# Backward attention on one core: six transposes of E a step, X copied by VectorE, row factors by Pool, G in half tiles, and Z's sum behind the products

## The chip, the cores and the metric

The kernel runs on one core of one Trainium2 chip. TensorE (PE) multiplies matrices, VectorE (DVE) and ScalarE (ACT) work elementwise and can read PSUM, where PE writes, GpSimd (POOL) works on SBUF, and SyncE (SP) issues most of the DMAs. The metric is the device time in microseconds of one execution; a comparison takes the median of several. Lines (L629) are those of the kernel before.

## The reference, cut to what matters

The function is a transformer block with a gate, and the reference returns its output and seven gradients. With S = 2048 rows, D = 512, H = 32 heads of 16, F = 1792:

```python
xn = _layernorm(x)
s  = attention(xn, wqkv) @ wo          # softmax over 2048 keys for each head
g  = _silu(mlp(_layernorm(xn)))
out = x + s * g
out, vjp = jax.vjp(f, x, wqkv, wo, w1, b1, w2, b2);  grads = vjp(grad_out)
```

For each head the attention stage needs E = exp(q k^T - bound), its row sums L, O = E v / L, and for the gradients G = E * (dO v^T) elementwise, from which dq, dk and dv come. E and G are 2048 x 2048 for each of 32 heads; nothing of them is stored in HBM.

## The kernel before

Three stages follow one another. `phase_pre` makes the normalized inputs, the projections, the MLP and the packed operands of the attention; `attention_core` (L543) makes O, dq and the key and value gradients; `phase3` makes the outputs and weight gradients. Outside the attention a scheduler orders the instructions; inside it (`manual_schedule`, L913) each engine runs them in the order in which the code emits them. The change touches the attention, and two lines of `phase_pre` that set a sign.

**Work and order.** A pair is two heads; there are 16. A block is a pair and a quarter (512) of the queries: 64 blocks. A step `g` is a block and 128 keys (`kb`, 0 to 15), so a block has 16 steps, and there are 1024. A block starts with the step in which `g % 16` is 0. The loop at L839 emits, for each step, pieces of several steps at once, so that the stages overlap:

- `emit_s` (L629, L635): two products `s` (one for each head) of step g+1, into PSUM tiles of `ps_st`, and ACT's exp of them into `et`, which holds four steps of E in bf16.
- `emit_d` (L647): two products `d` of step g into `ps_d`. Together, the four products of 32 rows each use all of PE's rows.
- `emit_mult` (L660): DVE multiplies `d` and `et` into `gts`, which holds two steps of G.
- `emit_T` (L694): PE transposes of E into a tile `tT` of the same pool `ps_st` (three tiles for s, s and tT). Of each group of four steps, three of four query blocks `qb` are transposed on PE, eight transposes in one step, in three of four steps. `emit_cT` (L704): ACT copies tT to an `ek` tile.
- `emit_dmat` (L674, L678): SP issues a DMA transpose of G for each two steps (`gk`), and one of the fourth query block of E for each four steps.
- `emit_x` (L719, L722, L725): six products of step g-1 that sum X over the 16 steps in one PSUM tile: the row sums (part "l"), E with keys and values ("e"), and G with keys ("g"). Each writes 32 (or 17) partitions: "l" and "e" fill the four column groups of PE, "g" uses two.
- `emit_xs` (L734): at the block's end, ACT copies X to SBUF. `emit_XT` (L744) transposes the copy on PE in float32, in step 2 of the next block (`FIN_AT`), and `emit_fin` (L756 to L782) works out the row factors: DVE copies XT (`xt`), takes the reciprocal of L (`rL`), and makes `dl` and `ndr`; POOL makes the weights `W1` and `W2`, O and dq.
- `emit_z` (L804): the sum Z of the key and value gradients, of a block that ended some steps earlier: step g works on what `g + ZOFF` names (ZOFF = -21). Half of its steps (part 0) multiply W2 with transposed G, half (part 1) W1 with transposed E: four products of 32 x 512 each step, one for each column group. `emit_acc` (L819) adds Z to `acc` on DVE, twice a block, in the steps where eight Z steps are complete; Z has one PSUM tile.

The order within a step is written out by hand:

```python
        emit_z(g + ZOFF)
        emit_acc(g + ZOFF)
        emit_s(g + 1, 0)
        emit_XT(g)
        emit_d(g, 0)
        emit_d(g, 1)
        emit_s(g + 1, 1)
        emit_mult(g)
        emit_fin(g)
        emit_T(g)
        ...
        emit_xs(g - 1)
        emit_cT(g)
        emit_dmat(g)
```

`load_ops` (L577) loads a pair's operands with three DMAs and two DMA transposes (`KVT`, `QDT`) on SP, spread over 16 steps of the pair before.

Of the kernel before, what the change touches and what calls it, by code (L numbers as in the profile page):

```python
# [58 lines left out]
def phase_pre(ctx, tc, k, A_x, A_wqkv, A_wo, B_w1, B_b1, B_w2, B_b2, grad_out, dbg):  # L59
# [3 lines left out]
    with ExitStack() as c1:  # L63
# [52 lines left out]
        with ExitStack() as c0:  # L116
# [5 lines left out]
            for i in range(2):  # L122
                nc.gpsimd.memset(NS[i][:, :, :, :, 0:1], 1.0)
# [28 lines left out]
            for t in range(NT):  # L152
                pq = psA.tile([128, 512], f32, name="pq", tag="mm")
                for ic in range(IC):
                    nc.tensor.matmul(pq[:], lhsT=xnT[:, ic, t * 128:(t + 1) * 128], rhs=wqkv_sb[:, ic, 0:D],
                                     start=(ic == 0), stop=(ic == IC - 1))
                nq = NQ[(t // 4) % 2]
                qpv = nq[:, :, t % 4, :, :]
                nc.scalar.copy(out=qpv[:, :, :, 1:17], in_=pq[:].rearrange("p (a j c) -> p a j c", a=NPAIR, j=2))
                qq = qpv[:, :, :, 1:17]  # L160
                sq = wk.tile([128, H, DH], f32, name="sqq")
                nc.gpsimd.tensor_tensor(out=sq[:].rearrange("p (a j) c -> p a j c", j=2), in0=qq, in1=qq, op=ALU.mult)
                qn2 = wk.tile([128, H], f32, name="qn2")
# [379 lines left out]
def attention_core(ctx, tc, NAT_s, NATQ_s, Oall, dQall, dKVT_out, ident_f32, ident_bf, npairs=16, nqc=4):  # L543
# [9 lines left out]
    gbp = sb("gbp", 7)  # L553
    ekp = sb("ekp", 19)
    xsp = sb("xsp", 1)
    finp = sb("finp", 1)
    wp = sb("wp", 2)
# [17 lines left out]
    acc = opnd.tile([128, 2, 512], f32, name="acc")  # L575

# [87 lines left out]
    def emit_dmat(g):  # L664
        a = a_unit(g)
        if a is None:
            return
        j, kb = a
        kc = kb // 4
        if kb % 2 == 1:  # L670
            h = (kb // 2) % 2
            if h == 0:
                blk[j]["Gk"][kc] = gbp.tile([128, 2, 16, 128], bf16, name="gk")
            nc.sync.dma_start_transpose(out=blk[j]["Gk"][kc][:, h], in_=st_gt[g][:].rearrange("k a h q -> k (a h q)"))  # L674
        if kb % 4 == 3:
            ek = ekp.tile([128, 8, 128], bf16, name="ek")
            blk[j]["Ek"][(kc, 3)] = ek
            nc.sync.dma_start_transpose(out=ek[:], in_=st_et[g][:, 3].rearrange("k a h q -> k (a h q)"))  # L678

    def t_unit(g):  # L680
        a = a_unit(g - 4)
        if a is None or a[1] % 4 == 3:
            return None
        return a[0], a[1] // 4, a[1] % 4

    def emit_T(g):
        u = t_unit(g)
        if u is None:
            return
        j, kc, qb = u  # L690
        et = st_et[j * 16 + kc * 4 + 3]
        t = ps_st.tile([128, 8, 128], bf16, name="tT", tag="st")
        for b in range(8):
            nc.tensor.transpose(t[:, b, :], et[:, qb, b // 2, b % 2, :], ident_bf[:])  # L694
        st_T[g] = t

    def emit_cT(g):
        u = t_unit(g)
        if u is None:
            return  # L700
        j, kc, qb = u
        ek = ekp.tile([128, 8, 128], bf16, name="ek")
        blk[j]["Ek"][(kc, qb)] = ek
        nc.scalar.copy(out=ek[:].rearrange("q a k -> q (a k)").bitcast(f32),  # L704
                       in_=st_T.pop(g)[:].rearrange("q a k -> q (a k)").bitcast(f32))
# [22 lines left out]
    def emit_xs(g):  # L728
# [4 lines left out]
        xs = xsp.tile([128, 512], f32, name="xs")  # L733
        nc.scalar.copy(out=xs[:], in_=blk[j].pop("X")[:])  # L734
# [12 lines left out]
    def emit_fin(g):  # L747
# [7 lines left out]
        xt = finp.tile([128, 4, 128], f32, name="xt")  # L755
        nc.vector.tensor_copy(out=xt[:], in_=XT[:])  # L756
        XTv = xt[:].rearrange("q b (r c) -> q b r c", r=4)
        W1 = wp.tile([128, 4, 2, 32], bf16, name="W1")
        W2 = wp.tile([128, 4, 2, 32], bf16, name="W2")
        nc.gpsimd.memset(W2[:, :, :, 0:16], 0.0)  # L760
# [16 lines left out]
        nc.gpsimd.tensor_tensor(out=t1[:], in0=XTv[:, :, 0:2, 0:16], in1=bc(dl[:]), op=ALU.mult)  # L777
        nc.gpsimd.tensor_tensor(out=t1[:], in0=XTv[:, :, 2:4, 1:17], in1=t1[:], op=ALU.subtract)
# [4 lines left out]
        blk[j]["W1"] = W1  # L783
        blk[j]["W2"] = W2

    def emit_z(g):
# [7 lines left out]
        for par in range(2):  # L794
            kc = 2 * kp + par
            if part == 0:
                W = blk[j]["W2"]
                mv = blk[j]["Gk"][kc][:].rearrange("q a (r h b) k -> q h b a r k", r=2, h=2)[:, :, qb]
            else:
                W = blk[j]["W1"]  # L800
                mv = blk[j]["Ek"].pop((kc, qb))[:].rearrange("q (a h) k -> q h a k", h=2)
            for hj in range(2):
                r = 64 * par + 32 * hj
                nc.tensor.matmul(Z[r:r + 32, :], lhsT=W[:, qb, hj, :], rhs=mv[:, hj],  # L804
                                 start=(part == 0 and qb == 0), stop=(part == 1 and qb == 3), skip_group_check=True,
                                 tile_position=(0, r))

    def emit_acc(g):
# [11 lines left out]
        if qc == nqc - 1:  # L820
            if kp == 0:
                cur["ob"] = outp.tile([128, 2, 512], bf16, name="ob")
            ob = cur["ob"]
            nc.gpsimd.tensor_copy(out=ob[:, kp, :], in_=av)
            if kp == 1:
                def store():
                    dv = dKVT_out[p * 64:(p + 1) * 64, :].rearrange("r (a b s) -> r a b s", a=2, b=2)
                    for b in range(2):
                        nc.sync.dma_start(out=dv[:, :, b, :], in_=ob[b * 64:(b + 1) * 64])
                late.append((cur["g"] + 2, store))  # L830

    FIN_AT = 2
    ZOFF = -21
# [5 lines left out]
    for g in range(NSTEP + 16 + 8):  # L839
# [11 lines left out]
        emit_z(g + ZOFF)  # L851
        emit_acc(g + ZOFF)
        emit_s(g + 1, 0)
        emit_XT(g)
# [118 lines left out]
```

## Time and profile before

| what | us |
|---|---|
| median of 3 runs | 2687.34 (2686.54 to 2688.6) |
| the profiled execution, its own time | 2689.98 |
| span of its instructions | 2688.2 |
| attention stage, from the first s to the last Z | 283 to 2085 |
| in that stage: PE busy | 1703.65 of 1802 |
| in that stage: ACT busy | 1530.79 |
| in that stage: DVE busy | 1434.70 |
| in that stage: POOL busy | 249.69 |

The stage is two thirds of the time, and TensorE's clock is granted in full in it (1.00). A line of a group of instructions reads: line, engine, operation, output <- inputs, shapes, count | busy us in total, mean ns of one | idle time of the engine just before them, and what ended most of it. A line of the timeline reads: start in us, duration in us, engine, line, operation, count, and in brackets the idle time before and what released it. Matmuls overlap in the records, so the start of one to the start of the next says more than a duration.

### The profile page before, as it was taken

How to read it: one execution, taken by the hardware profiler on the slowest of the kernel's cores; microseconds unless marked ns; L12 is line 12 of the kernel's file. 1: busy time of each engine (PE TensorE's matmuls, PEld its weight loads, DVE VectorE, ACT ScalarE, POOL GpSimd, SP SyncE). 2: the span in 40 equal slices, each digit the busy share in tenths (PEclk: the TensorE clock that was granted, in tenths of full speed). 3: DMA queues.
4: the chain of work that ended last, by engine and by line, in shares of the span. 5: the costliest groups of instructions: out<-in, count | busy, mean ns of one | idle time of the engine just before them, and what ended most of it. 6: DMA issues, size and time to landing. Idle time of an engine off the chain costs nothing. (4 is left out here: it accounts for less than half of the span.)

```text
span 2688.2 us, 61100 instructions
## 1 busy us (share of the span) xinstructions
PE 2294.1 (85%) x24005; PEld 1054.0 (39%) x24064; DVE 1898.4 (71%) x3190; ACT 1795.7 (67%) x3317; POOL 600.7 (22%) x990
## 2 busy tenths in 40 slices
PE   3788799999999999999999999999999656656967
PEld 2333244444444444444444444444444333322433
DVE  5766687878788778787787877778787368860144
ACT  3344688888888888888888888888887254430110
POOL 0434111011110111101111011110111258850034
PEclk8899899999999999999999999999999878878989
DMA  5343999999999999999999999999999633327331
GB/s 188 94 128 126 186 199 212 195 211 204 204 216 193 211 204 204 215 196 215 201 202 215 191 214 202 205 209 198 210 198 182 229 109 103 103 72 185 116 111 43
DMA packets 1564740, 477.08 MB, mean 177 GB/s; under 512 B 1484706, under 2 KB 1549603, under 8 KB 1564451
## 3 DMA queue, kind: packets, MB, share of 16 engines
q1 hardware_dynamic: 1491058, 419.56, 78.5%
q10 hardware_dynamic: 73392, 53.62, 6.5%
q8 instruction: 188, 3.08, 0.5%
q14 instruction: 102, 0.83, 0.1%
HBM read 65.41 MB, written 55.32 MB: 45 GB/s over the span
## 5 line engine op out<-in xcount | busy, mean ns | idle before, releaser
L660 DVE TENSOR_TENSOR gts<-d,et 128x512 bf16<-128x512 f32 x2048 | 1292.3, 683 | 364.1 <-PE s L629 200.1
L635 ACT ACTIVATE et<-s 128x512 bf16<-128x512 f32 x2048 | 1127.3, 596 | 247.9 <-PE s L629 136.7
L629 PE MATMUL s<-QDT,KVT 32*128 32x512 bf16 x2048 | 528.0, 386 | 17.7 <-DMA QDT<-Pad 16.1
L647 PE MATMUL d<-QDT,KVT 32*128 32x512 bf16 x2048 | 489.9, 383 | 54.0 <-DVE gts L660 53.7
L694 PE MATMUL tT<-ident_bf,et 128*128 128x128 bf16 x6144 | 475.2, 220 | 40.1 <-ACT ek L704 39.4
L704 ACT COPY ek<-tT 128x512 f32<-128x512 f32 x768 | 455.2, 593 | 0.5 <-PE tT L694 0.5
L694 PEld LDWEIGHTS <-et 128*128 128x128 bf16 x6144 | 354.2, 98 | 213.1 <-issue 199.2
L722 PE MATMUL X<-et,NAT 128*32 128x512 bf16 x2048 | 404.0, 392 | 0.0
L719 PE MATMUL X<-et,Lc 128*32 128x512 bf16 x2048 | 403.4, 391 | 0.0
L725 PE MATMUL X<-gts,NAT 128*17 128x512 bf16 x2048 | 393.4, 380 | 0.0
L629 PEld LDWEIGHTS <-KVT 32*128 32x128 bf16 x2048 | 145.3, 91 | 555.1 <-issue 523.8
L804 PE MATMUL Z<-ek,W 128*32 128x512 bf16 x2048 | 300.8, 380 | 0.0
L804 PE MATMUL Z<-gk,W 128*32 128x512 bf16 x2048 | 289.6, 380 | 1.3 <-DVE acc L819 1.3
L771 POOL TENSOR_TENSOR W<-NATQq,rL 128x128 bf16<-128x128 bf16 x64 | 25.7, 401 | 1178.3 <-DVE rL L766 1178.3
L804 PEld LDWEIGHTS <-W 128*32 128x32 bf16 x4096 | 199.7, 96 | 125.9 <-issue 31.2
L719 PEld LDWEIGHTS <-Lc 128*32 128x32 bf16 x2048 | 98.2, 93 | 139.0 <-issue 59.6
L647 PEld LDWEIGHTS <-KVT 32*128 32x128 bf16 x2048 | 96.0, 91 | 11.4 <-issue 11.4
L722 PEld LDWEIGHTS <-NAT 128*32 128x32 bf16 x2048 | 98.6, 93 | 0.0
L421 PE MATMUL dh_tp<-ident_bf,dh 128*128 128x128 bf16 x224 | 31.0, 278 | 77.9 <-DVE dh L418 75.5
L725 PEld LDWEIGHTS <-NAT 128*17 128x17 bf16 x2048 | 95.3, 90 | 0.0
L448 PE MATMUL ps_dw<-dm_all,hgc 128*128 128x512 bf16 x220 | 54.0, 402 | 29.6 <-DMA hgc<-HG_s 29.4
L427 PE MATMUL ps_dy<-w1T,dh1T 128*128 128x512 bf16 x208 | 67.8, 471 | 3.7 <-ACT dh1T L422 3.4
(197 smaller groups left out, 2442.2 us busy)
## 6 DMA issues: line engine op xcount, KB each, us to landing
gk<-gts SPq DMA_TRANSPOSE x512, 4.2
HG_s<-hg SPq DMA_DIRECT2D x16, 448.0 KB, 2.9
DH_s<-dh ACTq DMA_DIRECT2D x16, 448.0 KB, 2.5
NAT<-NAT_s SPq DMA_DIRECT2D x16, 264.0 KB, 3.3
GB_s<-gB ACTq DMA_DIRECT2D x16, 256.0 KB, 2.0
ek<-et SPq DMA_TRANSPOSE x256, 3.1
dKVT_s<-ob SPq DMA_DIRECT2D x32, 128.0 KB, 2.5
dhc<-DH_s ACTq DMA_DIRECT2D x2, 2048.0 KB, 13.7
```

The lines of the kernel that those rows point to most:

```text
L427: nc.tensor.matmul(ps[:], lhsT=dh1T[:, fc, :], rhs=w1T[:, fc, :], start=(fc == 0), stop=(fc == FC - 1))
L448: nc.tensor.matmul(ps[:], lhsT=hgc[:, t, :], rhs=dm_all[:, t, :], start=(t == 0), stop=(t == NT - 1))
L629: nc.tensor.matmul(s[:], lhsT=op["KVT"][r:r + 32, kb * 128:(kb + 1) * 128], rhs=op["QDT"][r:r + 32, qc * 512:(qc + 1) * 512], start=True, ...
L635: nc.scalar.activation(out=et[:, :, kb % 4, hj, :], in_=s[:].rearrange("k (b q) -> k b q", b=4), func=ACT.Exp)
L647: nc.tensor.matmul(d[:], lhsT=op["KVT"][r:r + 32, kb * 128:(kb + 1) * 128], rhs=op["QDT"][r:r + 32, qc * 512:(qc + 1) * 512], start=True, ...
L660: nc.vector.tensor_tensor(out=gts[:, kb % 2, hj, :].rearrange("k (b q) -> k b q", b=4), in0=st_d.pop((g, hj))[:].rearrange("k (b q) -> k b ...
L694: nc.tensor.transpose(t[:, b, :], et[:, qb, b // 2, b % 2, :], ident_bf[:])
L704: nc.scalar.copy(out=ek[:].rearrange("q a k -> q (a k)").bitcast(f32), in_=st_T.pop(g)[:].rearrange("q a k -> q (a k)").bitcast(f32))
L719: nc.tensor.matmul(X[64 + 32 * hj:96 + 32 * hj, :], lhsT=Lc[:], rhs=et[:, :, kb % 4, hj, :], start=(kb == 0), stop=False, skip_group_check ...
L722: nc.tensor.matmul(X[32 * hj:32 * hj + 32, :], lhsT=NATt[:, kb, hj, 1:33], rhs=et[:, :, kb % 4, hj, :], start=(kb == 0), stop=(kb == 15), ...
L725: nc.tensor.matmul(X[64 + 32 * hj:64 + 32 * hj + 17, :], lhsT=NATt[:, kb, hj, 0:17], rhs=st_gt[g][:, kb % 2, hj, :], start=False, stop=(kb ...
L804: nc.tensor.matmul(Z[r:r + 32, :], lhsT=W[:, qb, hj, :], rhs=mv[:, hj], start=(part == 0 and qb == 0), stop=(part == 1 and qb == 3), skip_ ...
```

## The change

Eight things change in `attention_core`:

- **Transposes.** Every step transposes three query blocks of its own 128 keys for two heads (six transposes), one step later than its exp, in place of eight on three steps of four. ACT copies 128 x 384 (float32 words) each step into a part of a larger `ek` tile (pool `ekc`, six tiles); the DMA transposes of the fourth query block have a pool of their own (`ekd`, six tiles).
- **Order of a step.** The transposes come first behind s and d, then XT, then Z, then the X products; before, Z came first in the step and XT between s and d. `emit_mult` and `emit_fin` come behind them, and `emit_acc` behind `emit_xs`.
- **X.** DVE copies it to SBUF, behind the products of its step; before, ACT did.
- **Row factors.** POOL makes `ndl` and `ndr`; the sign that `ndr` carried is put into the operands (the first column of NAT is -1, and u of the queries is positive).
- **W1 and W2** have two fixed tiles each, and the zeros of W2 are written once.
- **G** has a tile for each two steps (half of before's tile), 13 of them for 7; Z's part 0 uses eight products of 32 x 256 for four of 32 x 512.
- **Z** begins a step earlier in the block's count (ZOFF = -20).
- **The results** of each half of `acc` are stored by themselves: four DMAs of 64 KB a pair in place of two of 128 KB.

```diff
-                nc.gpsimd.memset(NS[i][:, :, :, :, 0:1], 1.0)
+                nc.gpsimd.memset(NS[i][:, :, :, :, 0:1], -1.0)
...
-                nc.vector.tensor_scalar(out=qpv[:, :, :, 0], in0=u[:].rearrange("p (a j) -> p a j", j=2), scalar1=-1.0, scalar2=None,
-                                        op0=ALU.mult)
+                nc.vector.tensor_copy(out=qpv[:, :, :, 0], in_=u[:].rearrange("p (a j) -> p a j", j=2))
...
-    gbp = sb("gbp", 7)
-    ekp = sb("ekp", 19)
+    gbp = sb("gbp", 13)
+    ekd = sb("ekd", 6)
+    ekc = sb("ekc", 6)
...
-            h = (kb // 2) % 2
-            if h == 0:
-                blk[j]["Gk"][kc] = gbp.tile([128, 2, 16, 128], bf16, name="gk")
-            nc.sync.dma_start_transpose(out=blk[j]["Gk"][kc][:, h], in_=st_gt[g][:].rearrange("k a h q -> k (a h q)"))
+            gk = gbp.tile([128, 2, 2, 4, 128], bf16, name="gk")
+            blk[j]["Gk"][kb // 2] = gk
+            nc.sync.dma_start_transpose(out=gk[:].rearrange("q r h b k -> q (r h b) k"), in_=st_gt[g][:].rearrange("k a h q -> k (a h q)"))
...
     def emit_T(g):
-        u = t_unit(g)
-        if u is None:
-            return
-        j, kc, qb = u
-        et = st_et[j * 16 + kc * 4 + 3]
-        t = ps_st.tile([128, 8, 128], bf16, name="tT", tag="st")
-        for b in range(8):
-            nc.tensor.transpose(t[:, b, :], et[:, qb, b // 2, b % 2, :], ident_bf[:])
+        a = a_unit(g)
+        if a is None:
+            return
+        kk = a[1] % 4
+        et = st_et[g]
+        t = ps_st.tile([128, 3, 2, 128], bf16, name="tT", tag="st")
+        for qb in range(3):
+            for hj in range(2):
+                nc.tensor.transpose(t[:, qb, hj, :], et[:, qb, kk, hj, :], ident_bf[:])
         st_T[g] = t
...
+        t = st_T.pop(g)
+        if kk == 0:
+            cur["ek"] = ekc.tile([128, 3, 4, 2, 128], bf16, name="ek")
+            blk[j]["Ek"][kc] = cur["ek"]
+        nc.scalar.copy(out=cur["ek"][:, :, kk].rearrange("q b h k -> q b (h k)").bitcast(f32),
+                       in_=t[:].rearrange("q b h k -> q b (h k)").bitcast(f32))
...
-        xs = xsp.tile([128, 512], f32, name="xs")
-        nc.scalar.copy(out=xs[:], in_=blk[j].pop("X")[:])
+        xs = xsp.tile([128, 512], f32, name="xs", tag="xs")
+        nc.vector.tensor_copy(out=xs[:], in_=blk[j].pop("X")[:])
...
-        dl = finp.tile([128, 4, 2, 1], f32, name="dl")
-        nc.vector.tensor_tensor(out=dl[:], in0=XTv[:, :, 2:4, 0:1], in1=rL[:], op=ALU.mult)
+        nc.gpsimd.tensor_tensor(out=W2[:, :, :, 16:32], in0=nqs, in1=bc(rL[:]), op=ALU.mult)
+        ndl = finp.tile([128, 4, 2, 1], f32, name="ndl")
+        nc.gpsimd.tensor_tensor(out=ndl[:], in0=XTv[:, :, 2:4, 0:1], in1=rL[:], op=ALU.mult)
         ndr = finp.tile([128, 4, 2, 1], f32, name="ndr")
-        nc.vector.scalar_tensor_tensor(out=ndr[:], in0=dl[:], scalar=-1.0, in1=rL[:], op0=ALU.mult, op1=ALU.mult)
-        nc.gpsimd.tensor_tensor(out=W2[:, :, :, 16:32], in0=nqs, in1=bc(rL[:]), op=ALU.mult)
+        nc.gpsimd.tensor_tensor(out=ndr[:], in0=ndl[:], in1=rL[:], op=ALU.mult)
...
+        for h in range(2 if part == 0 else 1):
+            for par in range(2):
+                kc = 2 * kp + par
+                for hj in range(2):
+                    r = 64 * par + 32 * hj
+                    if part == 0:
+                        nc.tensor.matmul(Z[r:r + 32, h * 256:(h + 1) * 256], lhsT=WT[j % 2][1][:, qb, hj, :],
+                                         rhs=blk[j]["Gk"][2 * kc + h][:, :, hj, qb, :],
+                                         start=(qb == 0 and h == 0), stop=False, skip_group_check=True, tile_position=(0, r))
...
-    ZOFF = -21
+    ZOFF = -20
...
-        emit_z(g + ZOFF)
-        emit_acc(g + ZOFF)
         emit_s(g + 1, 0)
-        emit_XT(g)
         emit_d(g, 0)
         emit_d(g, 1)
         emit_s(g + 1, 1)
-        emit_mult(g)
-        emit_fin(g)
-        emit_T(g)
+        emit_T(g - 1)
+        emit_XT(g)
+        emit_z(g + ZOFF)
         emit_x(g - 1, "l")
         emit_x(g - 1, "e")
         emit_x(g - 1, "g")
+        emit_mult(g)
+        emit_fin(g)
         emit_xs(g - 1)
-        emit_cT(g)
+        emit_acc(g + ZOFF)
+        emit_cT(g - 1)
         emit_dmat(g)
```

More of the change, by code (lines that the diff above doesn't have):

```diff
@@ L552, in attention_core @@
     gtp = sb("gtp", 3)
-    gbp = sb("gbp", 7)
-    ekp = sb("ekp", 19)
+    gbp = sb("gbp", 13)
+    ekd = sb("ekd", 6)
+    ekc = sb("ekc", 6)
     xsp = sb("xsp", 1)
     finp = sb("finp", 1)
-    wp = sb("wp", 2)
+    wp = sb("wp", 1)
     outp = sb("outp", 1)
@@ L575, in attention_core @@
     acc = opnd.tile([128, 2, 512], f32, name="acc")
+    WT = []
+    for i in range(2):
+        W1 = wp.tile([128, 4, 2, 32], bf16, name=f"W1_{i}")
+        W2 = wp.tile([128, 4, 2, 32], bf16, name=f"W2_{i}")
+        nc.gpsimd.memset(W2[:, :, :, 0:16], 0.0)
+        WT.append((W1, W2))
     def load_ops(p):
@@ L675, in emit_dmat @@
         if kb % 4 == 3:
-            ek = ekp.tile([128, 8, 128], bf16, name="ek")
+            ek = ekd.tile([128, 4, 2, 128], bf16, name="ekd")
             blk[j]["Ek"][(kc, 3)] = ek
[L678 to L684, printed above, removed]
+            nc.sync.dma_start_transpose(out=ek[:].rearrange("q a h k -> q (a h) k"), in_=st_et[g][:, 3].rearrange("k a h q -> k (a h q)"))
@@ L695, in emit_T @@
         st_T[g] = t
     def emit_cT(g):
-        u = t_unit(g)
-        if u is None:
+        a = a_unit(g)
+        if a is None:
             return
[L701 to L705, printed above, removed]
+        j, kb = a
+        kc, kk = kb // 4, kb % 4
+        t = st_T.pop(g)
@@ L754, in emit_fin @@
         XT = blk[j].pop("XT")
-        xt = finp.tile([128, 4, 128], f32, name="xt")
+        xt = xsp.tile([128, 4, 128], f32, name="xt", tag="xs")
         nc.vector.tensor_copy(out=xt[:], in_=XT[:])
         XTv = xt[:].rearrange("q b (r c) -> q b r c", r=4)
-        W1 = wp.tile([128, 4, 2, 32], bf16, name="W1")
-        W2 = wp.tile([128, 4, 2, 32], bf16, name="W2")
-        nc.gpsimd.memset(W2[:, :, :, 0:16], 0.0)
+        W1, W2 = WT[j % 2]
         st0 = qc * 4
@@ L776, in emit_fin @@
         t1 = finp.tile([128, 4, 2, 16], f32, name="t1")
-        nc.gpsimd.tensor_tensor(out=t1[:], in0=XTv[:, :, 0:2, 0:16], in1=bc(dl[:]), op=ALU.mult)
-        nc.gpsimd.tensor_tensor(out=t1[:], in0=XTv[:, :, 2:4, 1:17], in1=t1[:], op=ALU.subtract)
+        nc.gpsimd.tensor_tensor(out=t1[:], in0=XTv[:, :, 0:2, 0:16], in1=bc(ndl[:]), op=ALU.mult)
+        nc.gpsimd.tensor_tensor(out=t1[:], in0=XTv[:, :, 2:4, 1:17], in1=t1[:], op=ALU.add)
         rL4 = finp.tile([128, 4, 2, 1], f32, name="rL4")
@@ L782, in emit_fin @@
         nc.gpsimd.tensor_tensor(out=dQv, in0=t1[:], in1=bc(rL4[:]), op=ALU.mult)
-        blk[j]["W1"] = W1
-        blk[j]["W2"] = W2
     def emit_z(g):
@@ L793, in emit_z @@
         Z = blk[j]["Z"]
[L794 to L806, printed above, removed]
+        for h in range(2 if part == 0 else 1):
[7 more added lines that the diff above has]
+                                         start=(qb == 0 and h == 0), stop=False, skip_group_check=True, tile_position=(0, r))
+                    else:
+                        mv = blk[j]["Ek"][(kc, 3)][:] if qb == 3 else blk[j]["Ek"][kc][:, qb]
+                        nc.tensor.matmul(Z[r:r + 32, :], lhsT=WT[j % 2][0][:, qb, hj, :], rhs=mv[:, :, hj, :],
+                                         start=False, stop=(qb == 3), skip_group_check=True, tile_position=(0, r))
     def emit_acc(g):
@@ L820, in emit_acc, with store @@
         if qc == nqc - 1:
[L821 to L830, printed above, removed]
+            ob = outp.tile([128, 512], bf16, name="ob")
+            nc.gpsimd.tensor_copy(out=ob[:], in_=av)
+            def store():
+                dv = dKVT_out[p * 64:(p + 1) * 64, :].rearrange("r (a b s) -> r a b s", a=2, b=2)
+                for b in range(2):
+                    nc.sync.dma_start(out=dv[:, kp, b, :], in_=ob[b * 64:(b + 1) * 64, :])
+            late.append((cur["g"] + 2, store))
     FIN_AT = 2
-    ZOFF = -21
+    ZOFF = -20
     late = []
```

## The prediction

> **What bounds the kernel now.** First the page's busy times and groups: PE, VectorE (DVE) and ScalarE (ACT) are all 70 to 85% busy, and none is full.
>
> ```profile
> PE 2294.1 (85%) x24005; PEld 1054.0 (39%) x24064; DVE 1898.4 (71%) x3190; ACT 1795.7 (67%) x3317; POOL 600.7 (22%) x990
> ...
> L660 DVE TENSOR_TENSOR gts<-d,et 128x512 bf16<-128x512 f32 x2048 | 1292.3, 683 | 364.1 <-PE s L629 200.1
> L635 ACT ACTIVATE et<-s 128x512 bf16<-128x512 f32 x2048 | 1127.3, 596 | 247.9 <-PE s L629 136.7
> ...
> L694 PE MATMUL tT<-ident_bf,et 128*128 128x128 bf16 x6144 | 475.2, 220 | 40.1 <-ACT ek L704 39.4
> L704 ACT COPY ek<-tT 128x512 f32<-128x512 f32 x768 | 455.2, 593 | 0.5 <-PE tT L694 0.5
> ```
>
> PE's transposes wait for ACT's copies while ACT and DVE wait for PE: a ring, so I read it in the timeline. The attention stage runs from 283 to 2085 us, 64 blocks of 16 steps, 1.746 us a step, 27.94 us a block. Two steps inside a block:
>
> ```profile
> 1109.97 0.38 PE L629 MATMUL s<-QDT,KVT 32*128 32x512 bf16 x1
> ...
> 1110.30 0.62 PE L694 MATMUL tT<-ident_bf,et 128*128 128x128 bf16 x8
> 1110.39 1.08 ACT L635 ACTIVATE et<-s 128x512 bf16<-128x512 f32 x2
> ...
> 1111.36 0.59 ACT L704 COPY ek<-tT 128x512 f32<-128x512 f32 x1
> 1111.61 0.39 PE L629 MATMUL s<-QDT,KVT 32*128 32x512 bf16 x1
> ...
> 1112.01 0.61 PE L694 MATMUL tT<-ident_bf,et 128*128 128x128 bf16 x8
> ```
>
> The second transposes (1112.01) start 0.05 after the copy ends (1111.36 + 0.59), though PE could have begun at 1111.93. Three tiles of `ps_st` hold s, s and tT, so each waits for its predecessor's reader. Between starts, medians over steps 40 to 1000: s to exp 0.42, exp to exp 0.49, exp to copy 0.48; on PE, s to tT 0.32, tT to the L products 0.55, those to G's 0.23, G's (with half of Z beside them, then the other half) to the next s 0.53. PE alone needs 1.63 a step with transposes, 1.08 without; the ring through the copy (0.42+0.49+0.48+0.59+0.05, then 0.54+0.23+0.53) gives 3.33 for two, 1.67 each. In steps 5 to 15 the medians average 1.55: the ring, relieved each fourth step.
>
> The block's start is far worse: from step 0 to step 5, 10.5 us for five steps (medians 1.82, 2.34, 2.54, 1.27, 2.56). Its timeline:
>
> ```profile
> 1094.86 0.59 ACT L734 COPY xs<-X 128x512 f32<-128x512 f32 x1 [0.23 <-PE X L725]
> ...
> 1095.98 0.61 PE L694 MATMUL tT<-ident_bf,et 128*128 128x128 bf16 x8 [0.65 <-ACT ek L704]
> ...
> 1097.59 0.66 PE L744 MATMUL XT<-ident_f,xs 128*128 128x128 f32 x4
> ...
> 1098.17 0.39 PE L647 MATMUL d<-QDT,KVT 32*128 32x512 bf16 x2
> ...
> 1098.65 1.29 DVE L660 TENSOR_TENSOR gts<-d,et 128x512 bf16<-128x512 f32 x2 [1.90 <-PE s L629]
> ...
> 1102.01 0.37 PE L647 MATMUL d<-QDT,KVT 32*128 32x512 bf16 x1 [0.54 <-DVE gts L660]
> ```
>
> The copy of X puts tT 0.65 late; XT stands ahead of d, which comes 0.9 after s; then xt, rL, dl, ndr and acc stand ahead of the next products, and d and the second s behind it wait for those.
>
> **The change, part by part.**
>
> *Six transposes each step* (for eight on three of four). Their count stays; each group has one switch of 0.107 (0.551 minus 8 x 0.0555), now four for three. ACT's copy shrinks from 512 to 384 columns, between two forms of another copy out of PSUM:
>
> ```profile
> L422 ACT COPY dh1T<-dh_tp 128x512 bf16<-128x512 bf16 x48 | 26.6, 586 | 36.4 <-PE dh_tp L421 36.3
> ...
> L422 ACT COPY dh1T<-dh_tp 128x256 bf16<-128x256 bf16 x16 | 6.0, 375 | 1.3 <-PE dh_tp L421 1.2
> ```
>
> Half way, 0.48.
>
> *Z behind the transposes.* It no longer shares a slot with G's products. In the tail of the stage Z runs alone:
>
> ```profile
> 2079.04 0.40 PE L804 MATMUL Z<-gk,W 128*32 128x512 bf16 x4 [0.49 <-DVE acc L819]
> 2079.25 0.40 PE L804 MATMUL Z<-ek,W 128*32 128x512 bf16 x4
> ...
> 2080.55 0.40 PE L804 MATMUL Z<-ek,W 128*32 128x512 bf16 x4
> ```
>
> Eight groups of four start over 1.51, so 0.215 each. Without Z, in the first steps of the stage, s starts 0.315 after G's products. So tT to next s is 0.44+0.22+0.23+0.32 = 1.20; 1.18 where tT had waited and its weights were loaded (0.54 in place of 0.55 above, shortest 0.536). With 0.32 from s to tT, PE alone needs 1.51.
>
> The ring is now 0.42+0.49+0.48+0.48+0.05 = 1.92, plus 1.18: 3.10 for two steps, **1.55 each**, with no free fourth step. Against the 1.55 of before nothing is gained in mid-block. Sixteen such steps: 16 x 1.553 = 24.85 us.
>
> *G in half tiles.* Eight Z of 256 columns in place of four of 512, on 512 steps, 2048 more products and loads. At equal columns, nothing; if each product costs what it does in the tail (0.215/4), +0.215 a step. I take nothing: the four s and d start 3 ns apart, so a queued product needs no 54 ns to itself. Below nothing is excluded, as columns stay. The Trainium skill speaks against it (TensorE: Matmul & The Clock Gate, Back-to-back issue gap): a floor of about 25 ns per matmul, or about 62 where its sequencer decodes. By 62, eight would take 0.50, 144 us more in all; by 25, nothing. No row here decides below 54.
>
> *X by DVE, dl and ndr by Pool, XT behind the transposes.* Laid out with the durations above, t=0 at step 0's s. Products of a step start 0.52 after d and 0.61 apart. tT comes at 0.36, Z 0.78, L 1.0, G 1.23; X is complete at 1.23+0.38+0.05 = 1.66, its DVE copy (0.68, from xt's row) runs 1.75 to 2.43, and step 1's L products come at 2.56: no wait. Step 1's products start at 2.36, 0.3 late; d of step 2 (3.10) needs the first of them, ended 3.04: just in time. In step 2 tT starts at 3.46 (after the copy), and XT adds 0.59 in front of Z (from XT to d above): step 3 begins at 3.46+0.42+0.59+0.22+0.23+0.32 = 5.23, and step 4 on PE's own pace at 6.73, since that copy is long done. xt and rL end at 5.83, step 3's products go 5.85 to 7.14, acc to 7.75. In step 4 tT starts at 7.15; Z's next group wants PE at 7.57 and waits for acc till 7.80, as ps_z has one tile. Queued behind it on PE are the X products, which nobody wants yet, and step 5's s, for which ACT waits. Step 5 starts at 8.56 where five even steps take 7.75: **+0.81**. The second acc, at step 11, costs 0.14. Pool has W2 ready at 6.3 and W1 at 7.7 (rows of 0.40, two small ones of 0.24), before Z needs them at 7.6 and 9.3.
>
> DVE then does 32 x 0.61 + 4 x 0.68 + 0.2 = 22.4 a block, under 25.8; were that cover gone, X's copy would cost 0.68 x 64 = 44 us.
>
> *Transfers.* The same transposes, one gk half per two steps. Now the DMA stalls cost 0.36 a block (mean minus sum of the steps' medians, 27.94 - 27.58). A gts tile is reused six steps on: five steps less 1.28, 6.5 us, while gk lands a median 5.2, at worst 9.7, after its product. The block's start lost the slack it had, so I add 0.4 (bounds 0 and 1.0, three times the 0.36 rounded down). SP issues four dKVT stores of 64 KB a pair for two, some 0.6 us each, in idle queue time. The rings of gk (13) and ekd (6) come free in the step before, or half a step before, SP's transposes want them, so SP waits for the products as now. ACT's first copy of a group waits for the Z that reads its ek tile in the same step: that ends near 1.2, the copy starts at 1.39; were it later, the exps behind it would be late by as much.
>
> *The rest:* a copy for a scale at L168 (16 of 0.27) and a memset less on Pool: nothing, or 4 us less.
>
> Sum of a block: 24.85+0.81+0.14+0.36+0.40 = 26.56 against 27.94, -1.38; times 64, -88 us. The profiled execution took 2689.98 (span 2688.2), 2.6 above the median: 2602, and **2600** for the median. With DMA's bounds, 2573 to 2640.
>
> **Rivals.**
>
> *The ring loosens:* then PE's 1.51 bounds. 24.2+0.95+0.36 = 25.5 a block, -154 us, 2535. For it: 1.51 and 1.55 lie close. Against: every step now has a copy.
>
> *The new order does not do what it says:* X's copy on DVE pushes products and d back, and half of the 1.8 us hoped for at the block's start stays. +58: 2658. For it: margins of 0.06 and 0.13 above.
>
> *DMA becomes the wait.* From SP's own list of waits in the stage:
>
> ```profile
> SPq L674 <- DVE gts L660: 987.8, 470, 8.6
> ```
>
> For it: the page's DMA row reads 9 throughout the attention. Against: SP, before it issues a gk, sits 988 us waiting for products, so there is room between transfers. If one gts tile in four waits 0.7, 8 x 0.25 x 0.7 x 64 = 90 us, and the gain is gone: 2690 (between 2650 and 2695).
>
> *Slower: half tiles cost issue time.* If the eight products of Z's part 0 take 54 ns each, +0.215 on 512 steps, +110: 2710. It decides from 88/512 = 0.17 a step. Against: queued products start 3 ns apart.
>
> **How the numbers follow.** Forecast 0.55, ring loosened 0.12, half-kept start 0.10, DMA 0.13, half tiles 0.10. Against 2687, with 0.2% (5 us) what a measurement can tell: faster 0.55+0.12+0.09+0.08 = 0.84; same 0.01+0.03 = 0.04; slower 0.10+0.02 = 0.12. The range 2535 to 2695 leaves out the half-tile case and half of the loosened one, 0.18.
>
> **What would show it.** Right: tT starting 0.05 after each copy, about 1.55 between s in mid-block, 8.6 us for steps 0 to 4, no wait of X's L products for xs, a wait of Z for acc of some 0.2. Wrong: eight Z spread over 0.4 us; d waiting for gts after X's copy; many long waits of gts for gk; mid-block steps over 1.6.

## The result, and the profile after

| | before | after |
|---|---|---|
| median, us | 2687.97 (4 runs, 2686.54 to 2691.77) | 2641.46 (4 runs, 2639.53 to 2643.43) |
| profiled execution (span) | 2689.98 (2688.2) | 2641.33 (2639.6) |
| attention, first s to last s | 283.5 to 2071.2 | 283.0 to 2020.6 |
| block, mean | 27.94 | 27.17 |
| block, sum of the steps' medians | 27.58 | 25.68 |

The ratio is 0.9825, 95% interval 0.9808 to 0.9842: 46.5 us less, where 88 were forecast. The whole difference arises in the attention stage. The last two rows hold the story: a block in which nothing waits for a transfer became 1.90 us shorter, but the mean block only 0.77.

The page's busy times and the ring's groups after the change:

```profile
PE 2275.4 (86%) x26053; PEld 1097.6 (42%) x26112; DVE 1922.7 (73%) x3126; ACT 1765.4 (67%) x3509; POOL 613.4 (23%) x1056
...
L667 DVE TENSOR_TENSOR gts<-d,et 128x512 bf16<-128x512 f32 x2048 | 1308.9, 684 | 290.7 <-PE s L636 93.0
...
L695 PE MATMUL tT<-ident_bf,et 128*128 128x128 bf16 x6144 | 517.3, 221 | 0.3
...
L708 ACT COPY ek<-tT 128x384 f32<-128x384 f32 x1024 | 498.0, 486 | 2.5 <-PE tT L695 1.6
```

There are 2048 more PE products, as the half tiles need; VectorE is busier by 24 us, ScalarE and PE less than before. The copy takes 486 ns (forecast 480). The idle time ahead of the transposes' group fell from 40.1 to 0.3 us. That does not mean that they no longer wait for the copy: PE's records of the products ahead of them last until the transposes start, so no idle time is left to show. The starts in the timeline show it. Mid-block, from the changed kernel's timeline (start, duration, engine, line, operation):

```profile
693.20 0.40 PE L800 MATMUL Z<-gk,W 128*32 128x256 bf16 x8
...
693.43 0.38 PE L723 MATMUL X<-et,Lc 128*32 128x512 bf16 x2
...
694.39 1.08 ACT L642 ACTIVATE et<-s 128x512 bf16<-128x512 f32 x2
...
695.36 0.49 ACT L708 COPY ek<-tT 128x384 f32<-128x384 f32 x1
695.50 0.38 PE L636 MATMUL s<-QDT,KVT 32*128 32x512 bf16 x1
...
695.90 0.49 PE L695 MATMUL tT<-ident_bf,et 128*128 128x128 bf16 x6
```

The ring is there as drawn: the transposes (695.90) start 0.05 after the copy (695.36 + 0.49), though they could have followed s at 695.50 + 0.32. Eight Z products take 0.23 before the L products start; over all steps the median is 0.236 with eight products of 256 columns and 0.233 with four of 512. Mid-block steps without a sum of Z have medians of 1.59 and 1.53 in turn, 1.56 on average: 3.12 for two steps, where the ring was forecast at 3.10.

The block's start, same timeline; step 0's s is the one at 695.50 above:

```profile
697.29 0.69 DVE L738 COPY xs<-X 128x512 f32<-128x512 f32 x1
...
699.35 0.61 PE L748 MATMUL XT<-ident_f,xs 128*128 128x128 f32 x4
...
702.43 0.68 DVE L819 TENSOR_TENSOR acc<-Z,acc 128x512 f32<-128x512 f32 x1
...
703.16 0.40 PE L800 MATMUL Z<-gk,W 128*32 128x256 bf16 x8
...
703.93 0.39 PE L636 MATMUL s<-QDT,KVT 32*128 32x512 bf16 x1
```

X's copy begins 1.79 after step 0's s (forecast 1.75), XT comes behind the transposes of step 2, Z starts 0.05 after acc has ended (703.11), 0.58 behind the transposes' start where 0.42 is the rule: it waited 0.16. From 695.50 to 703.93 are 8.43 us for steps 0 to 4, against 8.56 forecast and 10.5 before.

So far all is as predicted. The waits for transfers are not. First the waits of before in its attention stage (engine, line, what it waited for, total, times, longest), then the same view of the changed kernel:

```profile
PE d L647 <- DVE gts L660: 53.7, 80, 1.9
...
DVE gts L660 <- DMA gk<-gts: 31.9, 23, 3.1
```

```profile
DVE gts L667 <- DMA gk<-gts: 75.5, 45, 4.2
PE d L654 <- DVE gts L667: 53.1, 56, 3.2
```

A product (gts) waits because the transfer that reads its old tile has not landed: 75.5 us where it was 31.9. Counting every product that starts within 0.15 of its tile's landing gives 87 of 509, before 41. They lie in the second and third quarters of each pair of heads (blocks 1 and 2 of each four), where the next pair's loads and the stores are issued: mean blocks 25.75, 28.21, 29.25 and 25.80 by quarter, before 27.63, 27.72, 29.18 and 27.65 (the first two and the last two blocks left out). One such wait, in the changed kernel's timeline:

```profile
971.81 6.01 SPq L680 DMA_TRANSPOSE gk<-gts  x2
...
977.28 0.60 ACT L642 ACTIVATE et<-s 128x512 bf16<-128x512 f32 x1
...
978.49 2.48 DVE L667 TENSOR_TENSOR gts<-d,et 128x512 bf16<-128x512 f32 x4 [2.94 <-DMA gk<-gts]
...
979.23 0.37 PE L654 MATMUL d<-QDT,KVT 32*128 32x512 bf16 x1 [1.99 <-DVE gts L667]
...
979.55 0.51 PE L695 MATMUL tT<-ident_bf,et 128*128 128x128 bf16 x6
...
981.30 0.82 PE L695 MATMUL tT<-ident_bf,et 128*128 128x128 bf16 x6
```

SP issues two gk behind three loads of the next pair (the last of them lands at 975.03) and is held 3.09 and 2.82 us by them, where a gk issued with no more than 1.5 us of the transfer before it pending (issued, not landed) holds it 1.63 (median; the least is 1.32). The first gk lands at 978.37, 6.6 us after its issue for a usual 4.3. The product waits 2.94 for it, d 1.99, and ACT behind d. The last line shows a second cost: 1.8 us behind the transposes at 979.55, the next six take 0.82, not 0.51. The profile by stretches (PE, PEld, DVE, ACT and POOL busy, then PE's granted clock, DMA share and GB/s):

```profile
979.00:980.70 1.70, 1.47 (x18) 0.64 (x17) 1.70 (x4) 0.97 (x2) 0.00 (x0) 1.00 1.12 248
980.70:982.00 1.30, 1.30 (x12) 0.67 (x10) 0.78 (x2) 0.60 (x2) 0.00 (x0) 0.50 0.49 113
982.00:983.50 1.50, 1.50 (x20) 0.48 (x18) 0.78 (x2) 0.85 (x2) 0.00 (x0) 0.50 1.27 288
```

The granted clock, 1.00 until 980.7, is 0.50 from there to 983.5 and full again after 985.5. The two steps behind the wait are 1.10 and 0.26 over their medians.

### The profile page after: what moved, and what is told of

Its sections match the earlier page's. It is cut to its first block, busy times and chain, and to the rows that moved or that the text cites. A ratio compares the mean times of both kernels' runs of the same rounds, so it can differ in the third digit from the quotient of the medians.

```text
span 2639.6 us, 65629 instructions
## 1 busy us (share of the span) xinstructions
PE 2275.4 (86%) x26053; PEld 1097.6 (42%) x26112; DVE 1922.7 (73%) x3126; ACT 1765.4 (67%) x3509; POOL 613.4 (23%) x1056
## 5 line engine op out<-in xcount | busy, mean ns | idle before, releaser
L667 DVE TENSOR_TENSOR gts<-d,et 128x512 bf16<-128x512 f32 x2048 | 1308.9, 684 | 290.7 <-PE s L636 93.0
L695 PE MATMUL tT<-ident_bf,et 128*128 128x128 bf16 x6144 | 517.3, 221 | 0.3
L708 ACT COPY ek<-tT 128x384 f32<-128x384 f32 x1024 | 498.0, 486 | 2.5 <-PE tT L695 1.6
L695 PEld LDWEIGHTS <-et 128*128 128x128 bf16 x6144 | 372.9, 98 | 239.7 <-issue 239.7
L654 PE MATMUL d<-QDT,KVT 32*128 32x512 bf16 x2048 | 426.5, 388 | 53.5 <-DVE gts L667 53.1
L636 PE MATMUL s<-QDT,KVT 32*128 32x512 bf16 x2048 | 438.7, 386 | 17.6 <-DMA QDT<-Pad 16.0
L636 PEld LDWEIGHTS <-KVT 32*128 32x128 bf16 x2048 | 110.4, 91 | 536.0 <-issue 535.3
L800 PE MATMUL Z<-gk,W 128*32 128x256 bf16 x4096 | 207.2, 279 | 12.8 <-DVE acc L819 4.1
L805 PE MATMUL Z<-ek,W 128*32 128x512 bf16 x1536 | 154.8, 392 | 0.7 <-POOL W L775 0.7
L800 PEld LDWEIGHTS <-W 128*32 128x32 bf16 x4096 | 73.6, 94 | 68.6 <-issue 17.7
L654 PEld LDWEIGHTS <-KVT 32*128 32x128 bf16 x2048 | 96.8, 91 | 1.8 <-issue 1.6
L805 PEld LDWEIGHTS <-W 128*32 128x32 bf16 x2048 | 52.8, 93 | 53.8 <-POOL W L775 1.0
```

What stands on the lines that cost most here:

```text
L636: nc.tensor.matmul(s[:], lhsT=op["KVT"][r:r + 32, kb * 128:(kb + 1) * 128], rhs=op["QDT"][r:r + 32, qc * 512:(qc + 1) * 512], start=True, ...
L654: nc.tensor.matmul(d[:], lhsT=op["KVT"][r:r + 32, kb * 128:(kb + 1) * 128], rhs=op["QDT"][r:r + 32, qc * 512:(qc + 1) * 512], start=True, ...
L667: nc.vector.tensor_tensor(out=gts[:, kb % 2, hj, :].rearrange("k (b q) -> k b q", b=4), in0=st_d.pop((g, hj))[:].rearrange("k (b q) -> k b ...
L695: nc.tensor.transpose(t[:, qb, hj, :], et[:, qb, kk, hj, :], ident_bf[:])
L708: nc.scalar.copy(out=cur["ek"][:, :, kk].rearrange("q b h k -> q b (h k)").bitcast(f32), in_=t[:].rearrange("q b h k -> q b (h k)").bitcas ...
L800: nc.tensor.matmul(Z[r:r + 32, h * 256:(h + 1) * 256], lhsT=WT[j % 2][1][:, qb, hj, :], rhs=blk[j]["Gk"][2 * kc + h][:, :, hj, qb, :], sta ...
```

## The experiments

All stand against before in their own session (2688.1 to 2689.7, 7 runs). **Theory:** the compute side gained as forecast; transfers that were hidden are not any more, since the steps became shorter and SP's queue and the DMA engines are the same. **Rivals:** the extra waits come from the changed order itself (tiles reused too soon), or the parts on the engines gained less than thought.

### Do the loads take the gain? (a_noload, b_noload)

The loads of all pairs but the first two are left out, with POOL's casts that belong to them, in the changed kernel and in before; the later pairs compute on old operands. The stores stay.

```diff
-            if kb == 0 and qc == 1 and p + 1 < npairs:
+            if kb == 0 and qc == 1 and p == 0:
```

> The changed kernel that loads operands for the first two pairs only and computes all later pairs with those (so the outputs are not the reference's; loads, casts and the KVT and QDT transposes of 14 pairs are left out). Theory (pair loads cause the stalls): a block costs its clean 25.7 us, 1.4 us less for 56 of 64 blocks and a little for the rest, 80 to 95 us in all, 2546 to 2562. Rival (average throughput): the left-out transfers are some 4 to 8 per cent of the traffic, so a third of the stalls goes at most, 2610 or more.

> The kernel before with the same loads left out (outputs not the reference's). Theory: it lost 0.36 us a block to them, 64 x 0.36 = 23 us at most, 2664 to 2670. Against the changed kernel without loads it then stands 110 to 122 us higher (27.58 against 25.7 a block), which is the gain of the change where no transfer is in the way. Rival (the stalls have another cause than the loads): no change, 2685 or more.

Measured: 2564.51 and 2660.99, so -77 us for the changed kernel and -28 for before (ratios to before 0.9543, 0.9527 to 0.9559, and 0.9901, 0.9887 to 0.9916). The waits of a_noload in the attention stage:

```profile
DVE gts L667 <- DMA gk<-gts: 16.8, 16, 2.7
```

With no loads in the way the waits fall from 75.5 to 16.8 us, the mean block is 25.87, and the change is worth 96.5 us; with them 46.5. **Some 50 us of its gain are given back to transfers.** The theory holds, though both times lie 3 us outside of the ranges given for them, so that the difference fell short of the 110 to 122 I had expected. That the order reuses its tiles too soon is out as the main cause, since the order and the stores are the same in a_noload. So are POOL's casts: in the changed kernel PE waits for POOL's weights 0.7 us in all.

### More room for the waiting product (gts4)

A fourth gts tile; to make room, dQall shares the memory of Oall, so one of the two is overwritten.

```diff
-    gtp = sb("gtp", 3)
+    gtp = sb("gtp", 4)
...
-        k.dQall = pO.tile([128, NT, D], bf16, name="dQall")
+        k.dQall = k.Oall
```

> The changed kernel with four gts tiles for three, so that a product waits for the transpose of eight steps ago and not of six; to make room, O and dQ share one SBUF tile (dQ overwrites O, so the outputs made from O are not the reference's; the same instructions run). Theory (the pair loads hold up the gk transposes in SP's queue, and the ring of gts is too short to bridge it): of the 1.49 us a block that the steps' means stand above their medians, at most 0.4 stay, 64 x 1.1 to 1.49 = 70 to 95 us, so 2545 to 2572. Rival (the DMA engines are full on average, and a longer ring only moves the wait): less than 20 us, 2620 or more, with the waits then in SP's queue or before Z.

Measured: 2607.56 (0.97, 0.9686 to 0.9715), -34: half of what the theory asked, well over the rival. The transfers then land later (median 7.95 us after the product, for 5.46) and 56 waits stay, most of them a quarter later: blocks 25.67, 26.18, 29.08, 25.88. The room moves part of the waits to a later place.

### Can the loads be spread? (spread, space, phase)

`spread` cuts each of the two 2048-column load transposes in four, one part every four steps, and puts the query half 16 steps later. `space` and `phase` only move the five or six load operations and the stores in the pair.

```diff
-            nc.sync.dma_start_transpose(out=t["KVT"][:].rearrange("r (m k) -> r m k", m=16),
-                                        in_=Pad[:].rearrange("q m j c -> q (m j c)"))
...
+                nc.sync.dma_start_transpose(out=t[dst][:, i * 512:(i + 1) * 512].rearrange("r (m k) -> r m k", m=4),
+                                            in_=Pad[:, i * 4:(i + 1) * 4].rearrange("q m j c -> q (m j c)"))
```

> The changed kernel with the loads of a pair spread: KVT and QDT in four transposes of 512 columns each, one every four steps, each behind a gk transpose and not ahead of it, the query half 16 steps later. Theory (a transpose of 3 us in SP's queue makes gk late by that): the longest hold-up falls from 3 us to under 1, and half to all of the stalls go, 45 to 90 us, 2550 to 2597. Rival (average throughput): same bytes and six more DMA instructions a pair, so no gain, 2635 to 2650.

Measured: 2661.41 (0.991, 0.9883 to 0.9936), 20 us **slower** than the changed kernel: the theory is refuted, and the rival, which expected no loss, was too low as well. SP's queue in `spread`:

```profile
779.05 1.63 SPq L680 DMA_TRANSPOSE gk<-gts  x1
780.73 1.27 SPq L598 DMA_TRANSPOSE KVT<-Pad  x1
782.10 1.66 SPq L680 DMA_TRANSPOSE gk<-gts  x1
```

A part with a quarter of the columns holds SP 1.27, a full one 1.7 (median). Eight parts cost a pair some 10.2 us for 3.4: +6.8. The waits (97.6 us) now lie in all four quarters (27.46, 28.05, 27.52, 27.30).

```diff
-        return [plain, ck, tk, cq, tq]
+        return [(10, plain_k), (14, ck), (18, tk), (26, plain_q), (30, cq), (34, tq)]
...
-            late.append((cur["g"] + 2, store))
+            late.append((cur["g"] + 3, store))
```

> The changed kernel with the same DMAs of a pair at other times: NAT at step 10 after the block's start, KVT at 18, NATQq and NATQd at 26, QDT at 34 (for 1, 9, 1, 17), the stores three steps behind their sum and not two; each stands at the start of a step of kb % 4 = 2, where SP has just issued one gk and owes no ekd. In the changed kernel SP holds 1.7 us for a gk, 1.3 for an ekd, 1.7 to 2.0 for KVT or QDT, and a gk is due each 3.1 us; so behind one gk a transfer of 1.7 us delays the next gk by 0.3, ahead of it by 1.7. Theory (SP's queue in order, and where the loads stand in it, makes the stalls): more than half of them go, 45 to 75 us, 2566 to 2597. Rival (the bytes count, wherever they stand): 2630 to 2650.

> The changed kernel with the loads kept close together, but each a step later (2, 6, 10, 14, 18 for 1, 5, 9, 13, 17; stores 3 steps behind for 2), so behind a gk and not ahead of it. Theory that the place against the next gk is what counts: most of the gain of the spaced loads, 2580 to 2605. Theory that the loads lie too close together for SP to work off one before the next comes (it gains 1.4 us in four steps): a third or less, 2615 to 2635. Rival (the bytes): 2630 to 2650.

(`phase` has the five operations at 2, 6, 10, 14 and 18, and the stores also one step later.) Measured: 2622.59 (0.9763, 0.9746 to 0.9781) and 2628.35 (0.9771, 0.9755 to 0.9787): -19 and -13. `space` lies between what its theory and its rival asked, and `phase` where the theory of loads too close together put it. So the place against the next gk counts; whether it helps to put the loads further apart as well is not shown, since the 6 us between the two lie within their spread. `space` has the lowest time here of the kernels that leave nothing out. Its waits are more (146) but shorter, and PE's clock seldom falls: three times, in the changed kernel ten.

### Which part of the loads? (no_kq)

The plain loads stay, the casts and the KVT and QDT transposes of later pairs are left out.

```diff
-                    late.append((g + 1 + 4 * i, f))
+                    if p == 0 or i == 0:
+                        late.append((g + 1 + 4 * i, f))
```

> The changed kernel that loads the later pairs' plain operands and leaves out their casts and the KVT and QDT transposes (outputs not the reference's). Between the changed kernel (2641) and a_noload (2564.5). If the two transposes cause the stalls (4 us of SP a pair against 1.7 for the plain loads): 2575 to 2590. If the plain loads do (528 KB at once beside a gk): 2620 to 2635.

Measured: 2594.85 (0.965, 0.9635 to 0.9664), -47 of the 77, 5 us above the range for the transposes as the cause. The two transposes with their casts are the larger part; the other 30 go to the plain loads, as far as the two simply add. The third quarter recovers (26.39); the second keeps 28.15, and there the plain loads lie.

### SP's issue time, or the DMA engines? (pool_dma, kq_act)

```diff
-            nc.sync.dma_start(out=t["NAT"][:].rearrange("q k j c -> q k (j c)"), in_=NAT_s[p])
+            nc.gpsimd.dma_start(out=t["NAT"][:].rearrange("q k j c -> q k (j c)"), in_=NAT_s[p])
```

and the same for the two NATQ loads and the stores.

> The changed kernel with its plain DMAs (three operand loads and four stores of dKVT a pair) issued by POOL and not by SP; the transposes stay on SP. In the changed kernel SP spends 1477 of 1650 us in its DMA instructions, of which these hold it about 4.3 us a pair (3 of 0.5 to 0.7, 4 of 0.66). Theory (SP's own time for issuing is what gk waits for: the spread loads added 6.4 us a pair to it and lost 20 us in all, the left-out loads took 5.7 us a pair from it and gained 77): 25 to 60 us less, 2580 to 2617. Rival (the 16 DMA engines are the limit, the same bytes give the same wait): 2630 to 2650.

Measured: 2653.69 (0.9867, 0.9852 to 0.9881), 12 us slower than the changed kernel; the theory that SP's issues alone are short is not borne out, and even the rival was too low. In its timeline, with the loads beside them and no longer ahead of them in SP's queue:

```profile
748.92 8.93 SPq L680 DMA_TRANSPOSE gk<-gts  x2
...
758.45 1.29 DVE L667 TENSOR_TENSOR gts<-d,et 128x512 bf16<-128x512 f32 x2 [3.17 <-DMA gk<-gts]
```

Two gk hold SP 8.93 us, and the first lands 9.4 us after its issue: the loads delay them from another queue as well. The loads themselves land 5.0 to 6.7 us after their issue (medians of the three), on SP 3.1 to 3.7. SP, rid of the plain DMAs, still spends 1462 us of the stretch from 300 to 1950 us in its DMA instructions, where the changed kernel spends 1475: its transposes hold it longer. But the run changed more than the place of issue: POOL's DMAs go through a queue that the profile lists as software_dynamic, SP's through one that it lists as hardware_dynamic. What that alone costs no run here shows.

In `kq_act` ScalarE issues the KVT and QDT transposes:

```diff
-            nc.sync.dma_start_transpose(out=t["KVT"][:].rearrange("r (m k) -> r m k", m=16),
+            nc.scalar.dma_start_transpose(out=t["KVT"][:].rearrange("r (m k) -> r m k", m=16),
```

> As the changed kernel, but ScalarE issues the two 2048-column transposes of a later pair's operands (KVT, QDT) instead of SyncE; what the DMA engines move stays the same. It asks which is the slow server: SyncE's time for issuing, or the 16 DMA engines. Dropping these two and their casts gave 47 us. Theory (SyncE's issue time is what is short): SyncE is rid of about 4 us a pair, so gts waits for gk less: about 8 such waits in the second quarters of the pairs instead of 27, blocks there near 26.4 us instead of 29.25. Rival (the DMA engines are short): 20 or more waits there, blocks of 28 us or more. ScalarE pays for it by the time an issue holds it: 30 issues of 1.3 to 2.0 us are 39 to 60 us if all lie on the ring, nothing if none does; so 2595 to 2655 by the theory and 2640 to 2700 by the rival, and where they overlap the count of waits decides.

Measured: 2775.58 (1.0318, 1.0301 to 1.0335), slower than before and outside of both expectations. Its timeline:

```profile
802.27 1.33 ACTq L597 DMA_TRANSPOSE KVT<-Pad  x1
803.65 1.08 ACT L642 ACTIVATE et<-s 128x512 bf16<-128x512 f32 x2 [6.44 <-issue]
804.30 0.58 PE L636 MATMUL s<-QDT,KVT 32*128 32x512 bf16 x1 [5.35 <-ACT et L642]
```

The issue takes 1.33, as I had assumed, but ACT stands still for 5.1 ahead of it, until SP's last gk has landed (802.20), and SP's next ekd (806.03) waits for KVT's landing (805.98) in turn: 15 times, up to 7.4 us, and as often for QDT's. In this program transposes of two queues follow one another. So ACT lost 159 us in 30 such places, and PE's granted clock is 0.95 over the stage. The blocks of the third quarter (counted from 0 in the expectation, the second) have one wait for gk left, which reads like the theory, but they are 31.82 us long, which gives SP the time back: **this run does not decide** between SP and the DMA engines.

### The three edits at the block's start (xs_act_nl, xt_early_nl, rows_dve_nl)

Each undoes one edit on top of a_noload, so that transfers don't blur it; they stand against its 2564.51.

```diff
-        nc.vector.tensor_copy(out=xs[:], in_=blk[j].pop("X")[:])
+        nc.scalar.copy(out=xs[:], in_=blk[j].pop("X")[:])
```

> The changed kernel without the later pairs' loads (as a_noload, outputs not the reference's), with X copied by ACT again. Against a_noload (2564.5). Theory (the ring through ACT's copy is what a step waits for, and X's copy stands in it; DVE has room): the next transposes wait 0.5 to 0.7 us longer, once a block, 30 to 45 us more, 2594 to 2610. Rival (X's copy pushes DVE's products back by as much as it frees ACT): no change, 2555 to 2575.

Measured 2605.06, **+40.5**: step 1 takes 2.40 in place of 1.53, since tT waits for the copy behind X's:

```profile
688.26 0.50 PE L695 MATMUL tT<-ident_bf,et 128*128 128x128 bf16 x6 [0.81 <-ACT ek L708]
```

```diff
         emit_s(g + 1, 0)
+        emit_XT(g)
         emit_d(g, 0)
...
         emit_T(g - 1)
-        emit_XT(g)
```

(XT ahead of d again, in place of behind the transposes.)

> The changed kernel without the later pairs' loads (outputs not the reference's), with XT ahead of d again. Against a_noload (2564.5). Theory (what stands ahead of d delays DVE's products, and with them d two steps on): 0.5 to 0.7 us a block, 30 to 45 us more, 2594 to 2610. Rival (XT costs PE its 0.59 us wherever it stands): no change, 2555 to 2575.

Measured 2605.97, **+41.5**: steps 2 to 4 take 2.43, 1.82 and 1.93 for 2.03, 1.53 and 1.75.

```diff
-        nc.gpsimd.tensor_tensor(out=ndl[:], in0=XTv[:, :, 2:4, 0:1], in1=rL[:], op=ALU.mult)
+        nc.vector.tensor_tensor(out=ndl[:], in0=XTv[:, :, 2:4, 0:1], in1=rL[:], op=ALU.mult)
```

and the same for ndr.

> The changed kernel without the later pairs' loads (outputs not the reference's), with ndl and ndr made by DVE and not by POOL. Against a_noload (2564.5). Theory (the two small operations, 0.17 and 0.27 us before, stand ahead of the products and of the sum of Z that the next Z waits for): 0.3 to 0.45 us a block, 19 to 28 us more, 2583 to 2593. Rival (DVE has room for them): no change, 2555 to 2575.

Measured 2596.69, **+32**, somewhat more than expected. In its timeline Z waits longer for acc:

```profile
692.86 0.68 DVE L819 TENSOR_TENSOR acc<-Z,acc 128x512 f32<-128x512 f32 x1
...
693.59 0.40 PE L800 MATMUL Z<-gk,W 128*32 128x256 bf16 x8 [0.36 <-DVE acc L819]
```

Step 4 takes 2.32 for 1.75. The three together make 114 us where the whole change without loads makes 96.5: they overlap, or its other parts cost some 17. No run separates these.

## Why the prediction was right, and what failed in it

**Right: sign, mechanism and nearly every term on the engines.** A block without waits for transfers: forecast 25.80 (24.85 + 0.81 + 0.14), measured 25.68. Its parts, forecast against measured medians: exp to exp 0.49, 0.493; copy 0.48, 0.487; tT to Z 0.42 to 0.44, 0.426 to 0.44; Z to the L products 0.22, 0.233; L to G 0.23, 0.216; G to the next s 0.32, 0.315; first five steps 8.56, 8.43. The block's start, 10.5 before, was to lose 1.9 and lost 2.1; undoing each of its three edits costs 32 to 41 us, 0.5 to 0.65 a block.

**Right: no gain by the ring's loosening, no loss by half tiles.** PE's own pace (1.51) is not reached, the ring holds mid-block steps at 1.56. Eight Z products cost 0.003 us a step more than four, not 0.215: 2 us in all, not 110. At 0.236 for eight, one has some 29 ns, below the 54 that decided that rival; the 0.50 for eight that the prediction also named did not come.

**Failed: "The block's start lost the slack it had, so I add 0.4".** The stalls on transfers are 1.49 a block (27.17 - 25.68), where I had 0.76 (0.36 + 0.40): 0.73 x 64 = 47 us, and the engines' terms give back 0.12 x 64 = 8; that makes 39 of the 41 us by which 2600 was missed. The step's bounds, nothing to 1.0 added, did not hold the measured 1.13 (1.49 - 0.36) either, so the inner range, 2573 to 2640 (2574 to 2638 if these bounds are worked out), ends below the measured 2641. The full range holds it only because it reaches up to the rivals. Three things were missed in this step.

First, I took SP's 988 us of waiting for products as room. They are not idle time. In the kernel before:

```profile
1109.12 1.20 SPq L829 DMA_DIRECT2D dKVT_s<-ob  x2
...
1110.40 1.82 SPq L674 DMA_TRANSPOSE gk<-gts  x1
1110.50 1.29 DVE L660 TENSOR_TENSOR gts<-d,et 128x512 bf16<-128x512 f32 x2 [0.42 <-PE s L629]
```

SP starts this gk 0.09 after the store ahead of it. Its own products had ended at 1108.88. Yet the list of waits puts 1.42 us down to it, up to the end of the products at 1110.50 + 1.29, which the next gk reads, while SP was issuing already. That is so for 469 of the 470 waits in that line: ahead of the 470, SP stood still for 226 us, not 988. In the stretch from 300 to 1950 us its DMA instructions, added up, take 1391 us before (84%) and 1475 after (89%), which leaves 259 and 175. The DMA rival's argument was the better one, its price (90 us) too high.

Second, I priced a gk by its landing after its product (5.2 median) and the shorter steps by the tile's reuse at 6.5, as if one transfer were late by itself. But a gk's issue holds SP longer the longer the transfer before it is pending: 1.69 us (median) at 1.5 to 2 us pending, 2.45 at 2.5 to 3, 3.76 at 4 to 6. From the landing ahead of it to its own, a gk issued straight behind another transfer takes 2.05 (median) and an ekd 1.0, so two gk and an ekd use 5.1 of the 6.2 us of four steps. Sixteen such groups and some 8.5 us of loads and stores make 90 us a pair, of the 103 that four blocks of 25.68 last: 88% full. This is an estimate, and on the high side: with more than 3 us pending, a gk lands 1.76 behind the landing ahead of it. By the estimate, what the loads put in the way drains at 1.1 us in four steps, so products wait again and again: 87 waits, not 41. `gts4` agrees with it: with a tile more the waits come a quarter later, and 34 us are won of the 77 that the loads cost.

Third, PE's clock. Ten times, nine of them right behind such a wait, PE's granted clock was half for 3.4 us (once 6.8); where the wait and what follows can be told apart, that is some 1.3 us each (1.10 + 0.26 above), so by estimate 10 to 13 us of the 47. Before had one such place, a_noload none.

**Open:** whether SP's issuing or the 16 DMA engines are the slower server. SP's hold grows with what is pending, so its time is not independent of theirs; pool_dma took the plain loads and the stores from SP and lost 12 us, which speaks for the engines, if POOL's kind of queue does not explain it; spread left the bytes as they were and added issues, and lost 20, which speaks for SP. Transposes from a second queue were tried (kq_act) and were held up by those of the first.

## What to carry to other kernels

When a compute stage gets shorter, price the transfers again as a server: add up the time from landing to landing that a whole period asks for and set it against the new, shorter period. The slack that one tile has by its age says little once the queue is nearly 90% full. A waiting time that a view gives for a queue is idle time only where the queue's instructions leave gaps: add these gaps up. The quickest test of whether transfers will take a gain back is to leave out the loads in both kernels and compare the two differences.

## What the runs showed of the hardware that was not expected

- A DMA transpose's hold on its issuing queue grows far less than its columns: 1.27 us for 512 (`spread`), 1.30 for the ekd of 1024, 1.63 for a gk of 2048 with up to 1.5 us pending (medians). Cutting the two of each pair in four, at other times, cost 20 us in the whole kernel.
- PE's granted clock fell to half in or within 4.5 us after each of the 35 idle gaps of over 2.5 us in the attention stage (all kernels here; 29 of the gaps in kq_act), 26 of the 51 of 1.4 to 2.0 us, and none of the 320 of 0.5 to 0.8. The Trainium skill (TensorE: Matmul & The Clock Gate, HAM oscillation) sets the limit for such a gap at some 3.4 us; these runs show it lower.
- Eight queued products of 256 columns in four column groups take 0.236 us until the products behind them start, some 29 ns each: within four they start 3 ns apart, and the second four 0.12 behind the first.
- Plain loads from POOL's queue took 5.0 to 6.7 us to land beside the transposes, 3.1 to 3.7 from SP's own queue (medians of the three).
